# The output product of a second FFN by seven products instead of eight, with its weights stationary

## Chip, cores, metric

One core of one Trainium2 chip. The metric is the device time of one execution in microseconds (us); the kernel before has a median of 1644.6 us.

## What is computed

A linear attention with a normalised output gives x of 4608 tokens x 512. Two feed-forward networks follow, each 512 to 2048 to 512, in float32. The change touches the second:

```python
def _moe2_ref(x, w_in, w_out):
    h = x @ w_in                      # (4608, 512) @ (512, 2048)
    beta = 1.0
    neg = h <= -beta
    pos = h >= beta
    g = np.where(pos, h, np.where(neg, 0.0, (h + beta) ** 2 / (4.0 * beta)))
    return (g @ w_out).astype(np.float32)   # (4608, 2048) @ (2048, 512)
```

## The kernel before

Tokens go in nine blocks of T = 512, the 2048 hidden columns in NF = 16 steps f of 128, eight pairs i of two steps. Every float32 product is made of three matmuls on float32r parts: an operand is split into hi (a ScalarE copy, rounded) and lo (a VectorE subtraction), and hi x hi, hi x lo and lo x hi are added in PSUM.

Nothing is issued in the order of the source. `op` (line 61) records each operation with its engine, a cost in us and a key; `new` (184) takes a tile from a ring of a fixed number of buffers, and a tile's operations wait for those of the tile that had its buffer. `Program.order` (78 to 128) then simulates the five queues (PE, ACT, DVE, POOL and SP, which issues all DMAs): a free engine starts the ready operation with the smallest key, and the kernel is written out in that order. PE's three matmuls are planned at 0.68 us, a VectorE operation C_TT at 0.602, a ScalarE one C_SB at 0.52, and after a DMA's issue cost 2.1 us pass.

In the first FFN (`ffn_step` with ph = 0, nine blocks) VectorE also decodes the 64-bit weights of the second FFN's first product (`prepare`, 314), forms the four sums S1 to S4 of their quarters for Strassen's scheme and stores all eight as tiles of 128 x 512 (256 hi columns, 256 lo) in DRAM (`wd`). Block 0 of the second FFN is done plainly (`ffn_step`, ph = 1): its first-product weights are fetched from `wd` (`fetch`, 660), its output weights decoded by `weight` (286) into the rings woh and wol, where they stay to the end.

The other eight blocks go in four groups g of two blocks ja and jb. `x_combinations` (669) loads x of both, forms and splits seven combinations (B11, T2, T1, B21, T3, T4, B22; 22 VectorE and 14 ScalarE operations, 10 loads). `ffn2_pair` (720) makes the h of two steps f and both blocks with seven products of six matmuls each into the banks h, o, m (Winograd's form: v1, u2, u3 gather the sums), its seven weight tiles streamed through the ring wih of 16. `ffn2_group` (788) applies `nonlinear` (761) to the four results, splits g into gh and gl, and multiplies with the resident weights by `ffn2_out` (772): for each f and each block four chunks of 128 tokens, g stationary, the weights moving, three matmuls each, summed over f in the banks acc0 to acc3. Since only four banks hold sums, the results of one block wait in ring raw while the other is summed, and the sums are made in halves of f (`partial`). Each result block of 128 tokens x 512 columns is stored in one DMA of 2 KB rows (`out_block`).

## Time and profile before

| what | value |
|---|---|
| median of three runs | 1644.6 us (1644.13 to 1646.16) |
| profiled execution | 1641.85 us, its span 1640.0 us |
| PE busy, matmuls | 1613.8 us (98%), 7696 |
| DVE, ACT busy | 1233.3 us (75%), 1100.8 us (67%) |
| moved by DMA | 180.34 MB, mean 110 GB/s |
| second FFN, four groups | from about 968 us to the end |

PE is TensorE's matmuls, PEld its weight loads, DVE VectorE, ACT ScalarE, SP the queue that issues DMAs (SPq). Times are us from the start of the span. [...] The duration of a matmul or an engine's operation includes its latency, and following ones overlap with it.

### The profile page before, as it was taken

The numbers are of one execution on the slowest core, as the hardware profiler recorded it, in microseconds if no ns is written. First come the engines' busy times: TensorE is split into PE (matmuls) and PEld (weight loads), VectorE is DVE, ScalarE is ACT, GpSimd is POOL, SyncE is SP. The second block draws the span as 40 slices with busy tenths as digits, with TensorE's granted clock in tenths as the row PEclk, the third lists the DMA queues.
The fourth block names the chain that finished last, engine by engine and source line by source line (L and its number), as shares of the span: only waits on it lengthen the run. The fifth ranks groups of instructions, "written<-read, shape, count | busy, mean of one in ns | idle before, by whom it ended". The sixth has DMA issues, their size and how long they took to land.

```text
span 1640.0 us, 21677 instructions
## 1 busy us (share of the span) xinstructions
PE 1613.8 (98%) x7696; PEld 1297.9 (79%) x7696; DVE 1233.3 (75%) x1968; ACT 1100.8 (67%) x1881; POOL 0.2 (0%) x4
## 2 busy tenths in 40 slices
PE   6999999999999999999999999999999999999999
PEld 3665788888888888888888878888888888888887
DVE  5999999999999999999999734346534653465343
ACT  6988888888888888888888635345434543454343
POOL 0000000000000000000000000000000000000000
PEclk9999999999999999999999999999999999999999
DMA  8966303030211203021434644235423542344211
GB/s 276 308 213 201 129 27 110 20 116 21 76 41 46 89 27 109 14 90 39 148 109 151 211 139 127 79 103 167 126 80 102 166 126 82 101 137 128 78 33 52
DMA packets 107116, 180.34 MB, mean 110 GB/s; under 512 B 18240, under 2 KB 42688, under 8 KB 107008
## 3 DMA queue, kind: packets, MB, share of 16 engines
q1 hardware_dynamic: 107008, 178.96, 34.8%
q8 instruction: 61, 1.00, 0.3%
q14 instruction: 47, 0.39, 0.1%
HBM read 142.35 MB, written 36.57 MB: 109 GB/s over the span
## 4 chain that ended last, share of the span: by engine, by line
PE 84%; DVE 7%; ACT 4%; DMA 3%; issue 1%; SPq 0%; ACTq 0%; DVEq 0%
PE h L586 7%; PE o L735 7%; PE h L587 7%; PE h L588 7%; PE acc L782 7%; PE acc L784 7%; PE acc L783 7%; PE acc L635 6%; PE acc L636 6%; PE acc L637 6%; PE h L735 5%; PE m L735 5%; PE acc L633 2%; DVE u L212 1%; DMA io<-x2d 1%; DMA raw<-in_w_dram 1%
## 5 line engine op out<-in xcount | busy, mean ns | idle before, releaser
L586 PE MATMUL h<-xh,wih 128*128 128x512 f32 x640 | 256.8, 401 | 4.0 <-DVE t L212 2.0
L587 PE MATMUL h<-xl,wih 128*128 128x512 f32 x640 | 249.3, 389 | 0.0
L588 PE MATMUL h<-xh,wil 128*128 128x512 f32 x576 | 224.3, 389 | 0.0
L782 PE MATMUL acc<-woh,gh 128*128 128x512 f32 x512 | 199.5, 390 | 1.5 <-ACT ah L198 1.5
L635 PE MATMUL acc<-gh,woh 128*128 128x512 f32 x512 | 200.0, 391 | 0.0
L636 PE MATMUL acc<-gh,wol 128*128 128x512 f32 x512 | 199.3, 389 | 0.0
L784 PE MATMUL acc<-woh,gl 128*128 128x512 f32 x512 | 199.2, 389 | 0.0
L783 PE MATMUL acc<-wol,gh 128*128 128x512 f32 x512 | 199.2, 389 | 0.0
L637 PE MATMUL acc<-gl,woh 128*128 128x512 f32 x512 | 199.2, 389 | 0.0
L212 DVE SCALAR_TENSOR_TENSOR u<-u,r 128x512 f32<-128x512 f32 x272 | 187.0, 688 | 2.1 <-ACT r L198 0.9
L203 DVE TENSOR_TENSOR gl<-u,gh 128x512 fp32r<-128x512 f32 x208 | 143.0, 689 | 41.5 <-ACT gh L198 33.6
L198 ACT ACTIVATE gh<-u 128x512 fp32r<-128x512 f32 x208 | 130.9, 631 | 64.1 <-PE acc L640 20.0
L586 PEld LDWEIGHTS h<-xh,wih 128*128 128x128 f32 x640 | 120.1, 188 | 36.4 <-DVE t L212 3.2
L587 PEld LDWEIGHTS h<-xl,wih 128*128 128x128 f32 x640 | 120.2, 188 | 27.1 <-issue 3.2
L198 ACT ACTIVATE r<-u 128x512 f32<-128x512 f32 x144 | 91.1, 633 | 65.6 <-DVE u L208 65.6
L588 PEld LDWEIGHTS h<-xh,wil 128*128 128x128 f32 x576 | 108.2, 188 | 22.8
L198 ACT ACTIVATE u<-ah,absb 128x512 f32<-128x512 f32 x144 | 117.7, 818 | 0.0
L198 ACT ACTIVATE u<-kv 128x512 f32<-128x512 f32 x64 | 40.4, 632 | 114.9 <-DVE kv L743 102.2
L782 PEld LDWEIGHTS acc<-woh,gh 128*128 128x128 f32 x512 | 96.1, 188 | 22.5 <-ACT ah L198 2.7
L635 PEld LDWEIGHTS acc<-gh,woh 128*128 128x128 f32 x512 | 96.1, 188 | 21.4 <-ACT ah L198 1.0
L784 PEld LDWEIGHTS acc<-woh,gl 128*128 128x128 f32 x512 | 96.1, 188 | 20.1 <-DVE gl L203 0.2
L198 ACT ACTIVATE t<-h,na 128x512 f32<-128x512 f32 x144 | 112.0, 778 | 0.0
(163 smaller groups left out, 3107.5 us busy)
## 6 DMA issues: line engine op xcount, KB each, us to landing
wih<-wd SPq DMA_DIRECT2D x256, 256.0 KB, 2.8
raw<-in_w_dram SPq DMA_DIRECT2D x64, 512.0 KB, 4.3
wd<-raw SPq DMA_DIRECT2D x48, 256.0 KB, 2.2
io<-x2d SPq DMA_DIRECT2D x44, 256.0 KB, 2.9
x2d<-io SPq DMA_DIRECT2D x36, 256.0 KB, 2.3
raw<-in_qT_dram SPq DMA_DIRECT2D x56, 128.0 KB, 3.0
raw<-in_kv_dram SPq DMA_DIRECT2D x12, 512.0 KB, 5.0
out_dram<-a SPq DMA_DIRECT2D x18, 256.0 KB, 2.1
```

The source lines that it names most:

```text
L198: op(ACT, cost, key, lambda: nc.scalar.activation(out=out(), in_=in_(), func=func, **{k: v() if callable(v) else v for k, v in kw.items()} ...
L212: op(DVE, C_STT if callable(add) else C_TT, key, lambda: nc.vector.scalar_tensor_tensor(out=out(), in0=x(), scalar=add() if callable(add) ...
L586: nc.tensor.matmul(out=h(), lhsT=whi()[:, hc], rhs=xh(), start=(p == 0), stop=False)
L587: nc.tensor.matmul(out=h(), lhsT=whi()[:, hc], rhs=xl(), start=False, stop=False)
L588: nc.tensor.matmul(out=h(), lhsT=wlo()[:, lc], rhs=xh(), start=False, stop=(p == KT - 1))
L635: nc.tensor.matmul(out=o(), lhsT=wohi()[:, c], rhs=gh(), start=first, stop=False)
L636: nc.tensor.matmul(out=o(), lhsT=wolo()[:, c], rhs=gh(), start=False, stop=False)
L637: nc.tensor.matmul(out=o(), lhsT=wohi()[:, c], rhs=gl(), start=False, stop=last)
L735: nc.tensor.matmul(out=bank(), lhsT=l, rhs=r[k](), start=(start and k == 0 and m == 0), stop=(k == 1 and m == 2), skip_group_check=True,)
L782: nc.tensor.matmul(out=o(), lhsT=gh()[:, c], rhs=wohi(), start=first, stop=False)
L783: nc.tensor.matmul(out=o(), lhsT=gh()[:, c], rhs=wolo(), start=False, stop=False)
L784: nc.tensor.matmul(out=o(), lhsT=gl()[:, c], rhs=wohi(), start=False, stop=last)
```

## The change

In the four groups the second product is made by the same scheme as the first. Over the pairs i, the two steps f of a pair and the two halves of the 512 output columns are the quarters of the weights; the two blocks and the two steps are the quarters of g. So all eight pairs' g are kept: `ffn2_in` now ends with the four results of a pair in ring slots of woh and wol (the plain block's weights are no longer needed there), as B11, T1, T2 and B21. `ffn2_out` runs after all eight `ffn2_in` of the group: seven products, each over eight pairs with two halves of 128 output columns, the weights stationary and streamed from a new DRAM tensor `wod`, hi and lo of the g combination moving (made from the kept g just before, in ring raw; T3, B22 and T4 are formed anew each time in ring dec). The result comes out with columns on partitions and tokens along them; `put` turns it in squares of 32 x 32 on VectorE and stores it in four DMAs of 32 partitions. For the squares to join up, the output columns of the weights are permuted (`swapped`, `straight`), and the plain block's result is put back by its PSUM copy.

`prepare_out` takes the place of `weight(1, f, 1, ...)`: it decodes two steps' output weights, splits them as before, stores A11, A12 and A22 from the parts, forms and splits S1 to S4 and stores these. Ring wil gets 12 instead of 16 buffers; two tiles of a new ring ow hold the first four steps' lo of the first FFN and later the turned results. The combinations of x get keys spread over a longer stretch. The rest of the removed code (`ffn2_pair`, `ffn2_group`, the old `ffn2_out`, `stream`) is in the listing above. The diff, cut to its core:

```diff
+    wod = dram.tile([NPAIR, 8, P, T], F32, name="wod")
-        "wih": NF, "wil": NF, "woh": NF, "wol": NF + 1, "raw": 4, "dec": 2, "io": 3, "xh": KT, "xl": KT,
+        "wih": NF, "wil": NF - 4, "ow": 2, "woh": NF, "wol": NF + 1, "raw": 4, "dec": 2, "io": 3, "xh": KT, "xl": KT,
...
+    def swapped(x, h=None):
+        x = x.rearrange("p (a m j) -> p m a j", a=4, m=4)
+        return x if h is None else x[:, 2 * h:2 * h + 2]
+    def straight(x, m=4):
+        return x.rearrange("p (m a j) -> p m a j", m=m, a=4)
+    def prepare_out(i, key):
+        ts, his, los = [], [], []
+        for n in range(2):
+            f, k = 2 * i + n, key + n
+            raw, t = new("raw", k, I64, (P, DM)), new("dec", k, I32)
+            hi, lo = new("woh", k, F32R), new("wol", k, F32R)
+            load(k - 4, raw, w2[f, 1], 1.4)
+            decode(k, raw, t, new(f"kv{n}", 0.5 * (k - NS1) - 20 + NS1, I32))
+            op(ACT, C_SB, k, lambda t=t, hi=hi: nc.scalar.activation(
+                out=straight(hi()), in_=swapped(t().bitcast(F32)), func=AF.Copy), [t], [hi])
+            op(DVE, C_TT, k, lambda t=t, hi=hi, lo=lo: nc.vector.tensor_tensor(
+                out=straight(lo()), in0=swapped(t().bitcast(F32)), in1=straight(hi().bitcast(F32)), op=ALU.subtract
+            ), [t, hi], [lo])
+            wsb[1, f, 1] = (hi, lo)
+            ts.append(t)
+            cs = (A11, A21) if n == 0 else (A12, A22)
+            done = prog.buf(None)
+            def go(hi=hi, lo=lo, cs=cs, n=n):
+                for h in range(n + 1):
+                    for o, x in ((0, hi), (HW, lo)):
+                        nc.sync.dma_start(out=wod[i, cs[h], :, o:o + HW], in_=x().bitcast(F32)[:, h * HW:(h + 1) * HW])
+            op(SP, 0.7 * (n + 1), k + 1.5, go, [hi, lo], [done])
+            for c in cs[:n + 1]:
+                wods[i, c] = done
...
+        k = key + 2
+        s12, s34 = new("a1", k), new("a2", k)
+        (a, b), q = ts, (slice(0, HW), slice(HW, T))
...
+        def add(out, oh, x, y, alu, reads):
+            op(DVE, 0.34, k, lambda: nc.vector.tensor_tensor(
+                out=half(out, oh), in0=x(), in1=y(), op=alu), reads, [out])
+        add(s12, 0, lambda: whole(a, 1), lambda: whole(b, 1), ALU.add, [a, b])
+        add(s12, 1, lambda: half(s12, 0), lambda: whole(a, 0), ALU.subtract, [s12, a])
+        add(s34, 0, lambda: whole(a, 0), lambda: whole(a, 1), ALU.subtract, [a])
+        add(s34, 1, lambda: whole(b, 0), lambda: half(s12, 1), ALU.subtract, [b, s12])
+        for t, ring, c in ((s12, "a3", S1), (s34, "a4", S3)):
+            hi = new(ring, k, F32R)
+            op(ACT, C_SB, k + 0.5, lambda t=t, hi=hi: nc.scalar.activation(
+                out=hi(), in_=t(), func=AF.Copy), [t], [hi])
+            op(DVE, C_TT, k + 0.5, lambda t=t, hi=hi: nc.vector.tensor_tensor(
+                out=t().bitcast(F32R), in0=t(), in1=hi().bitcast(F32), op=ALU.subtract
+            ), [t, hi], [t])
...
-                t = new(("r", "r", "a1", "a2")[m] if ph else "io", k)
-                activate(k, t, o, cost=C_PS)
+                t = new("ow" if ph else "io", k)
+                if ph:
+                    op(ACT, C_PS, k, lambda t=t, o=o: nc.scalar.activation(
+                        out=swapped(t()), in_=straight(o()), func=AF.Copy), [o], [t])
+                else:
+                    activate(k, t, o, cost=C_PS)
...
+    PRODUCTS = ((0, A11, B11), (1, S2, T2), (2, S1, T1), (1, S3, T3), (0, A12, B21), (2, S4, B22), (1, A22, T4))
+    PAIR, PROD = 1.75, 2.0
...
+    def x_combinations(g, key, span):
...
+        at = [0]
+        def now():
+            at[0] += 1
+            return key + span * at[0] / 22
...
+    def pe_product(cost, key, bank, w, m, hi, lo, start, stop):
+        def mm():
+            wh, wl = (w()[:, o + m * P:o + (m + 1) * P] for o in (0, HW))
+            for n, (l, r) in enumerate(((wh, hi), (wh, lo), (wl, hi))):
+                nc.tensor.matmul(
+                    out=bank(), lhsT=l, rhs=r(), start=(start and n == 0), stop=(stop and n == 2), skip_group_check=True,
+                )
+        op(PE, cost, key, mm, [w, hi, lo], [bank])
...
+    def ffn2_in(g, i, key):
+        odd = (i + (g == 0)) % 2
+        a, b, c = banks = [new(r, key) for r in ("h", ("acc0", "o")[odd], ("acc1", "m")[odd])]
+        v1, u2, u3 = new("t", key), new(("kv0", "a1")[odd], key), new(("kv1", "a2")[odd], key)
+        def product(n):
+            bank, wc, xn = PRODUCTS[n]
+            w = fetch(wd, wds, i, wc, key - 4 + 0.1 * n, 4)
+            for k in range(2):
+                pe_product(0.68, key + 0.1 * n, banks[bank], w, k, xc[g, xn][0][k], xc[g, xn][1][k], n < 3 and k == 0, k == 1)
+        product(0)
+        activate(key, v1, a, cost=C_PS)
+        product(1)
+        arith(key, u2, v1, b)
+        product(2)
+        product(3)
+        arith(key, u3, v1, b)
+        product(4)
+        arith(key, u3, u3, c)
+        product(5)
+        product(6)
+        k = key + 0.8
+        g11, g12 = (new("woh", k + 0.1 * n) for n in range(2))
+        g22, g21 = (new("wol", k + 0.1 * n) for n in range(2))
+        nonlinear(a, g11, k)
+        nonlinear(u3, g22, k)
+        arith(key, u2, u2, c)
+        arith(key, v1, v1, b)
+        nonlinear(u2, g12, k)
+        nonlinear(v1, g21, k)
+        arith(k + 0.2, g12, g12, g11, ALU.subtract)
+        arith(k + 0.2, g22, g22, g12, ALU.subtract)
+        return {B11: g11, T1: g12, T2: g22, B21: g21}
...
+    def ffn2_out(g, gs, key):
+        banks = [[new(r, key + PROD * n) for r in rs]
+                 for n, rs in enumerate((("acc2", "acc3"), ("o", "m"), ("acc0", "acc1")))]
+        v1, u2, u3 = [[new(r, key + PROD * n) for r in rs]
+                      for n, rs in enumerate((("a3", "a4"), ("gh", "gh"), ("gl", "gl")))]
+        def product(n):
+            bank, wc, xn = PRODUCTS[n]
+            for i in range(NPAIR):
+                k = key + PROD * n + PROD / NPAIR * i
+                w = fetch(wod, wods, i, wc, k - 4, 4)
+                x = new("raw", k - 0.5, F32R, (P, 2 * T))
+                hi, lo = Half(x, slice(0, T)), Half(x, slice(T, 2 * T))
+                e, ke = gs[i].get(xn), k - 0.6
+                if e is None:
+                    l, r, alu = {T3: (T2, B11, ALU.subtract), B22: (T2, T1, ALU.add), T4: (B21, T2, ALU.subtract)}[xn]
+                    l, r, e = gs[i][l], gs[i][r], new("dec", k - 0.5)
+                    op(DVE, C_TT, ke, lambda l=l, r=r, e=e, alu=alu: nc.vector.tensor_tensor(
+                        out=e(), in0=l(), in1=r(), op=alu), [l, r], [e])
+                op(ACT, C_SB, ke, lambda e=e, hi=hi: nc.scalar.activation(
+                    out=hi(), in_=e(), func=AF.Copy), [e], [hi])
+                op(DVE, C_TT, ke, lambda e=e, hi=hi, lo=lo: nc.vector.tensor_tensor(
+                    out=lo(), in0=e(), in1=hi().bitcast(F32), op=ALU.subtract), [e, hi], [lo])
+                for m in range(2):
+                    pe_product(0.68, k, banks[bank][m], w, m, hi, lo, n < 3 and i == 0, i == NPAIR - 1)
+            return key + PROD * (n + 1)
+        def put(j, h, cs, key):
+            w = new("ow", key, shape=(P, 2 * T))
+            for m in range(2):
+                op(DVE, C_TT, key, lambda m=m: nc.vector.transpose(
+                    out=w().rearrange("p (b m j) -> p m b j", m=2, j=32)[:, m], in_=cs[m]()), [cs[m]], [w])
+            stored = prog.buf(None)
+            def go():
+                for n in range(4):
+                    nc.sync.dma_start(
+                        out=out[j * T:(j + 1) * T, n * P + h * D:n * P + (h + 1) * D].rearrange("(b i) c -> i b c", i=32),
+                        in_=w()[n * 32:(n + 1) * 32].rearrange("p (b c) -> p b c", c=D),
+                    )
+            op(SP, 2.8, key, go, [w], [stored])
...
+        a, b, c = banks
+        k = product(0)
+        for m in range(2):
+            activate(k, v1[m], a[m], cost=C_PS)
+        k = product(1)
+        for m in range(2):
+            arith(k, u2[m], v1[m], b[m])
+        product(2)
+        k = product(3)
+        for m in range(2):
+            arith(k, u3[m], v1[m], b[m])
+        for m in range(2):
+            arith(k, u3[m], u3[m], c[m])
+        put(jb, 1, u3, k + 1)
+        k = product(4)
+        put(ja, 0, a, k)
+        k = product(5)
+        for m in range(2):
+            arith(k, u2[m], u2[m], c[m])
+        put(jb, 0, u2, k + 1)
+        k = product(6)
+        for m in range(2):
+            arith(k, v1[m], v1[m], b[m])
+        put(ja, 1, v1, k + 0.5)
...
-        weight(1, f, 1, NS1 + f - 0.95 + 2.9)
+        if f % 2 == 0:
+            prepare_out(f // 2, NS1 + f - 0.5)
         for n in range(2):
-            plain[f, n] = fetch(f // 2, (A11, A21)[f % 2] + n, NS1 + f - 3 + 0.4 * n, 0)
+            plain[f, n] = fetch(wd, wds, f // 2, (A11, A21)[f % 2] + n, NS1 + f - 3 + 0.4 * n, 0)
...
-        s0 = NS1 + NF + 2 * NF * g
-        x_combinations(g, s0 - 6)
-        for i in range(NPAIR):
-            stream(g, i, s0 + (i // 4) * NF + 2.92 * (i % 4) - 7)
-        ffn2_group(g, s0)
+        s0 = NS1 + NF + (NPAIR * PAIR + 7 * PROD) * g
+        x_combinations(g, s0 - (8 if g else 6), 6 if g else 4)
+        units = [ffn2_in(g, i, s0 + PAIR * i) for i in range(NPAIR)]
+        ffn2_out(g, units, s0 + NPAIR * PAIR)
```

## Rows read from the trace of the kernel before

**Rows 1.** The page's busy times (us, share of the span, instructions).

```profile
PE 1613.8 (98%) x7696; PEld 1297.9 (79%) x7696; DVE 1233.3 (75%) x1968; ACT 1100.8 (67%) x1881; POOL 0.2 (0%) x4
```

**Rows 2.** The page's chain that ended last, by engine.

```profile
PE 84%; DVE 7%; ACT 4%; DMA 3%; issue 1%; SPq 0%; ACTq 0%; DVEq 0%
```

**Rows 3.** Stage windows, the groups: length; busy us (instructions) by engine; clock; DMA share, GB/s.

```profile
968.00:1114.00 146.00, 144.86 (x639) 119.54 (x638) 70.42 (x106) 64.38 (x109) 0.00 (x0) 1.00 0.41 119
1114.00:1278.00 164.00, 163.38 (x722) 134.95 (x721) 85.02 (x131) 74.13 (x127) 0.00 (x0) 1.00 0.41 119
1278.00:1442.00 164.00, 163.13 (x720) 134.78 (x719) 84.80 (x130) 73.89 (x126) 0.00 (x0) 1.00 0.40 119
1442.00:1606.00 164.00, 164.00 (x725) 135.51 (x724) 80.28 (x123) 71.25 (x122) 0.00 (x0) 1.00 0.29 86
```

**Rows 4.** Waits of PE from 960 us on: us in total, times, longest.

```profile
PE acc L782 <- ACT ah L198: 1.5, 2, 0.9
PE o L735 <- DVE kv L743: 1.1, 1, 1.1
```

**Rows 5.** Chain in order of time: start, us, what (two pieces of a group).

```profile
1154.61 1.36 PE h L735 x6
1155.97 1.36 PE o L735 x6
```

**Rows 6.** Groups of instructions, second FFN's matmuls: count, busy us, mean ns, idle before.

```profile
L782 PE MATMUL acc<-woh,gh 128*128 128x512 f32 x512 | 199.5, 390 | 1.5 <-ACT ah L198 1.5
...
L735 PE MATMUL o<-xh,wih 128*128 128x512 f32 x256 | 89.3, 390 | 1.1 <-DVE kv L743 1.1
...
L735 PE MATMUL m<-xl,wih 128*128 128x512 f32 x64 | 24.9, 389 | 0.0
```

**Rows 7.** Timeline of DVE, first FFN: start, us, line, operation.

```profile
312.17 0.69 DVE L203 TENSOR_TENSOR gl<-u,gh 128x512 fp32r<-128x512 f32 x1
312.77 0.68 DVE L212 SCALAR_TENSOR_TENSOR u<-u,r 128x512 f32<-128x512 f32 x1
...
320.71 0.42 DVE L331 TENSOR_TENSOR raw<-dec 128x256 f32<-128x256 f32 x1
321.05 0.75 DVE L212 SCALAR_TENSOR_TENSOR r<-t,na,r 128x512 f32<-128x512 f32 x1
```

**Rows 8.** A window of the first FFN, columns as in rows 3.

```profile
270.00:360.00 90.00, 90.00 (x428) 73.73 (x427) 87.78 (x143) 76.37 (x131) 0.00 (x0) 1.00 0.18 59
```

**Rows 9.** SP's issues by line: ns min/median/max; landing likewise, us (of line 662).

```profile
L662 SPq DMA_DIRECT2D wih<-wd x256: 319/320/1270, 798.6 to 1570.8; - x128
DMA to landing us min/median/max: 2.3/2.8/5.1
...
L434 SPq DMA_DIRECT2D kv<-kvd x28: 512/602/612, 121.7 to 584.1; - x28
```

**Rows 10.** Windows with the fullest DMA and with kv's reload, columns as in rows 3.

```profile
60.00:80.00 20.00, 20.00 (x137) 12.73 (x135) 20.00 (x33) 19.91 (x38) 0.00 (x0) 1.00 0.99 330
...
311.00:312.00 1.00, 1.00 (x6) 0.83 (x5) 1.00 (x3) 1.00 (x3) 0.00 (x0) 1.00 0.48 106
```

**Rows 11.** Timeline at the end of the span, all engines.

```profile
1634.14 2.73 DVE L840 TENSOR_TENSOR a<-a,acc 128x512 f32<-128x512 f32 x4 [2.27 <-PE acc L784]
...
1634.85 2.37 SPq L799 DMA_DIRECT2D out_dram<-a x4
...
1635.75 0.39 PE L784 MATMUL acc<-woh,gl 128*128 128x512 f32 x1
```

**Rows 12.** Windows around the plain block, columns as in rows 3.

```profile
880.00:900.00 20.00, 20.00 (x90) 16.57 (x89) 17.95 (x30) 15.98 (x29) 0.00 (x0) 1.00 0.61 185
900.00:920.00 20.00, 19.08 (x85) 15.48 (x84) 18.50 (x30) 16.36 (x31) 0.00 (x0) 1.00 0.81 271
920.00:940.00 20.00, 20.00 (x90) 16.57 (x89) 13.75 (x22) 11.62 (x20) 0.00 (x0) 1.00 0.58 176
940.00:960.00 20.00, 20.00 (x90) 16.58 (x89) 4.85 (x7) 6.83 (x11) 0.00 (x0) 1.00 0.36 105
```

More of the change, by code (lines that the diff above doesn't have):

```diff
@@ L679, in x_combinations @@
             k = key + 0.1 * n
-            hl = [[new("wil", k + 6 + 0.01 * (2 * m + i), F32R) for i in range(2)] for m in range(2)]
-            xc[g, c] = hl
+            xc[g, c] = [[new("wil", k + 0.01 * (2 * m + i), F32R) for i in range(2)] for m in range(2)]
         for n, c in enumerate((B21, T3, T4, B22)):
@@ L684, in x_combinations, with read, sub @@
             xc[g, c] = [[Half(w, slice(i * T, (i + 1) * T)) for i in range(2)] for w in wholes]
+        at = [0]
+        def now():
+            at[0] += 1
+            return key + span * at[0] / 22
+        def read(j, p):
+            k = key + span * at[0] / 22
+            t = new("io", k)
+            load(k - 1, t, x2d[j, p], reads=[x2s[j, p]])
+            return t
+        def sub(out, x, y):
+            op(DVE, C_TT, now(), lambda: nc.vector.tensor_tensor(
+                out=out(), in0=x(), in1=y(), op=ALU.subtract), [x, y], [out])
@@ L698, in split @@
-            def split(c, e, i=i, k=k):
-                x_split(e, xc[g, c][0][i], xc[g, c][1][i], k + 0.01 * c)
-            b11, b12 = fetch(ja, i, 0), fetch(jb, i, 1)
-            split(B11, b11)
-            t1, t2 = (new("dec", k + 6 + 0.1 * n) for n in range(2))
+            b11, b12 = read(ja, i), read(jb, i)
+            split(B11, b11, i)
+            t1, t2 = (new("r", key + i + 0.1 * n) for n in range(2))
             sub(t1, b12, b11)
-            b22 = fetch(jb, 2 + i, 2)
+            b22 = read(jb, 2 + i)
@@ L706, in x_combinations @@
             sub(t2, b22, t1)
-            split(T2, t2)
-            split(T1, t1)
-            b21 = fetch(ja, 2 + i, 3)
-            split(B21, b21)
+            split(T2, t2, i)
+            split(T1, t1, i)
+            b21 = read(ja, 2 + i)
+            split(B21, b21, i)
             sub(b12, b22, b12)
-            split(T3, b12)
-            t4 = new(f"kv{i}", k + 4)
+            split(T3, b12, i)
+            t4 = new("t", key + 1 + 0.1 * i)
             sub(t4, b21, t2)
-            late.append((split, fetch, t4))
@@ L716, in x_combinations @@
-        for i, (split, fetch, t4) in enumerate(late):
-            split(T4, t4)
-            split(B22, fetch(jb, 2 + i, 4))
-    def ffn2_pair(g, i, key):
-        banks = [new(r, key) for r in ("h", "o", "m")]
-        a, b, c = banks
-        v1, u2, u3 = new("t", key), new("kv0", key), new("kv1", key)
-        def product(n, bank, wc, xn, start):
-            w = ws[g, i, wc]
-            xh, xl = xc[g, xn]
-            def mm():
-                for k in range(2):
-                    hi, lo = (w()[:, o + k * P:o + (k + 1) * P] for o in (0, HW))
-                    for m, (l, r) in enumerate(((hi, xh), (hi, xl), (lo, xh))):
-                        nc.tensor.matmul(
-                            out=bank(), lhsT=l, rhs=r[k](), start=(start and k == 0 and m == 0),
-                            stop=(k == 1 and m == 2), skip_group_check=True,
-                        )
-            op(PE, 1.36, key + 0.01 * n, mm, [w, *xh, *xl], [bank])
-        def add(out, x, bank):
-            op(DVE, C_TT, key, lambda: nc.vector.tensor_tensor(
-                out=out(), in0=x(), in1=bank(), op=ALU.add), [x, bank], [out])
-        product(0, a, A11, B11, True)
-        product(1, b, S2, T2, True)
-        product(2, c, S1, T1, True)
-        activate(key, v1, a, cost=C_PS)
-        add(u2, v1, b)
-        product(3, a, A12, B21, False)
-        product(4, b, S3, T3, False)
-        add(u3, v1, b)
-        add(u3, u3, c)
-        product(5, b, A22, T4, False)
-        product(6, c, S4, B22, False)
-        add(v1, v1, b)
-        add(u2, u2, c)
-        return (a, u2), (v1, u3)
@@ new lines, in x_combinations @@
+            late.append(t4)
+        for i, t4 in enumerate(late):
+            split(T4, t4, i)
+            split(B22, read(jb, 2 + i), i)
+    def pe_product(cost, key, bank, w, m, hi, lo, start, stop):
[6 more added lines that the diff above has]
+        op(PE, cost, key, mm, [w, hi, lo], [bank])
@@ L770, in nonlinear @@
         return out
-    def ffn2_out(e, f, o4, key, first, last):
-        gh, gl = new("gh", key - 0.8, F32R), new("gl", key - 0.8, F32R)
-        activate(key - 0.8, gh, e)
-        subtract(key - 0.8, gl, e, gh)
-        wohi, wolo = wsb[1, f, 1]
-        for m in range(4):
-            o = o4[m]
-            def out_mm(m=m, o=o):
-                c = slice(m * P, (m + 1) * P)
-                nc.tensor.matmul(out=o(), lhsT=gh()[:, c], rhs=wohi(), start=first, stop=False)
-                nc.tensor.matmul(out=o(), lhsT=gh()[:, c], rhs=wolo(), start=False, stop=False)
-                nc.tensor.matmul(out=o(), lhsT=gl()[:, c], rhs=wohi(), start=False, stop=last)
-            op(PE, 0.68, key, out_mm, [wohi, wolo, gh, gl], [o])
@@ L851 @@
     for f, half in order:
-        weight(0, f, half, early.get((f, half), f - 2.8 + half * 2.7))
+        weight(f, half, early.get((f, half), f - 2.8 + half * 2.7))
     kv_batch(0, -30, 0.01)
```

118 lines of the change are left out of this document (40 added, 78 removed).

## Prediction

> **What bounds the kernel now.** I read the busy shares first: PE is busy 98% of the span [rows 1]. The chain that ended last says the same, PE 84%, DVE 7% [rows 2]. Then the stages: in the four groups of two token blocks (968 us to the end) PE has 144.86 of 146, 163.38 of 164, 163.13 of 164 and 164.00 of 164 us, while DVE has 70 to 85 and ACT 64 to 74 [rows 3]. The view of PE's waits from 960 us on has two lines, 2.6 us together [rows 4]. So in the stage that the change rewrites nothing but the number of matmuls sets the time, and what one costs is read from the chain: six take 1.36 us, 0.2267 us each [rows 5]. (The mean of 390 ns in a group row is latency; they overlap.)
>
> **Matmuls, the gain.** A group now does 8 pairs x 7 products x 6 = 336 matmuls of the first product (nine groups of line 735, 1344 = 4 x 336) and 16 rows of g x 2 blocks x 4 x 3 = 384 of the second (lines 782 to 784, 3 x 512 = 4 x 384) [rows 6]. The change makes the second 7 products x 8 pairs x 2 halves x 3 = 336. That is 48 fewer in each group, 192 x 0.2267 = **43.5 us**, all on the path that sets the end. A group's PE work is then 672 x 0.2267 = 152.3 us, half first product, half second (76.2 each).
>
> **VectorE in a group.** Durations of 0.69 us overlap too; ops that follow without a gap start 0.60 us apart [rows 7]. Before, a group has 130 of them: 8 x 13 in the pairs, 4 for the partial sums, 22 in x_combinations. The change drops 32 (gl) and 4, adds 56 (lo of each unit of pair and product), 24 (T3, B22, T4 are not kept), 16 (g12 and g22 by differences), 10 for the banks and 8 transposes: 208 x 0.603 = 125.4 of 152.3 us. In the first half it is 88 ops, 53 of 76 us. In the second half, with the 22 for the next group, 120 ops, 72.4 of 76.2 us: 95%. That can be carried: from 270 to 360 us PE was busy all 90 us with DVE at 87.8 of 90 [rows 8], under the same planner. Its costs are near the trace's: 0.68 for three matmuls (0.680), 0.602 for a VectorE op. ScalarE goes from 126 to 144 ops; at 73.9/126 = 0.59 us each [rows 3] that is 85 of 152 us, no bound.
>
> The transpose stands nowhere in this trace. [...] I take a full op, 0.603, since it moves the same 128x512 elements. [...]
>
> Price of stalls: the second half buffers four units ahead (ring raw, 4), 5.4 us, and the waits on a bank have a whole product (10.9 us) between writer and reader. In the first half c must be read between products 3 and 5, two VectorE ops in 1.36 us, but the planner puts products of the next pair there, whose banks alternate. Loads of x2 come later than planned on a fuller queue. Before lost 0.0 to 1.1 us per group; I take 1.25, **5 us** in all, between 0 and the DVE rival below.
>
> **Streams.** Each group fetches 112 tiles of 256 KB instead of 56, one per 1.36 us. With 2.6 MB of x2 and 2.1 MB of results that is 34.1 MB in 152.3 us, 224 GB/s; 119 GB/s cost a share of 0.41 [rows 3], so 0.77. The queue issues one in 0.32 us and it lands in 2.8 [rows 9]; the ring wih holds 16 tiles, 21.8 us ahead. Hidden, at zero, while a fetch is less than 20 us late.
>
> **Stores.** Eight stores of 128 rows of 2 KB per group become 16 of 32 partitions, each of 512 pieces of 256 B. The nearest row is the reload of kv in 256 B pieces: 0.60 us per issue [rows 9], 106 GB/s at a share of 0.48 [rows 10], a full-share rate of 221 GB/s. A put of 512 KB is then 2.4 us of the engines and 2.4 us of SP's queue; upper bound 1.2 us per issue (double pieces), 4.8. All fetches queued behind wait that long, far less than 20 us. But that row reads DRAM; a write to DRAM in 256 B pieces is not in the trace. [...]
>
> **The tail.** Now the last matmul starts at 1635.75 and the span ends at 1640.0: 4.25 us [rows 11]. After, both banks of the last product end together: VectorE adds twice and transposes twice (last one done 0.43 + 3 x 0.603 + 0.09 = 2.3 us after that start), then four issues of 0.60 (the fourth starts 1.9 later), 2.2 us to land as now, 0.9 to the end: 7.3. With 1.2 us per issue and 5 us of landing, 12. Growth 3 to 8, I take **5**.
>
> **The plain block (about 895 to 968 us).** prepare_out adds per pair two full and four half VectorE ops, 8 x (2 x 0.603 + 4 x 0.34) = 20.5 us, and two ScalarE ops. From 880 to 960 DVE has 55.1 of 80 us [rows 12], so 75.6: it fits. Its DMAs are the tighter part: seven tiles per pair, 56 x 256 KB = 14.7 MB in 1 KB rows, on top of the 14.7 MB that those 80 us move now (mean 184 GB/s): 368 GB/s, more than the 330 GB/s seen at a share of 0.99 [rows 10]. 3.0 MB, 9 us, spill. They may: the stores are read only in group 0's second half, 76 us on, and the plain fetches run up to 16 tiles (43 us) ahead. What is queued behind on SP are weight loads, and an ACT decode that waits for a late one holds the nonlinear op behind it, then PE. Between 0 and 9, I take **3**. Group 0's x combinations share VectorE with this, and are late next.
>
> At nothing: the wider "ow" tiles and the ring wil of 12 in the first FFN (the early weights only change homes, and its stage is bound by PE and DVE at 90.0 and 87.8 of 90 [rows 8]); "ow" for the plain block's four results (two wait for a store, while acc2 and acc3 are next needed 76 us later).
>
> **The sum.** The profiled execution takes 1641.85 us (span 1640.0); it lies 2.75 under the median of the runs, 1644.6. 1641.85 - 43.5 + 5 + 5 + 3 = 1611.4; on the median, **1614**.
>
> **Rivals.**
> 1. VectorE bounds the second half. If the 22 combination ops stay where their keys put them (s0-8, the last four products), these products carry 32 + 24 + 22 + 12 = 90 ops, 54.3 us, against 43.5 of PE: 10.8 over, less up to 5.4 of buffer, in three groups: 16 to 32 us, 1624 to 1645, centre 1632. For it: DVE at 95%, late x2 loads, dear transposes. Against: the planner starts any ready operation on an idle engine, and in the first three products VectorE has 24 x (1.36 - 0.60) = 18 us free for 13.3 of combinations.
> 2. The plain block starves: the 9 us of spill and a disordered queue stop PE, and group 0 starts late by VectorE as well: 10 to 20 us beyond the sum, 1621 to 1631. For it [rows 10, 12]; against, the look-ahead.
> 3. Stores of 256 B pieces saturate the DMA engines; slower than before. Without the puts a group wants 32 MB, at 290 GB/s 110 of 152 us; 42 us are left, 10.5 per put (50 GB/s). Beyond that point every us counts four times per group; at 13.5 us per put (39 GB/s) 4 x 12 = 48 us, 1662. Against it is the 221 GB/s of the reload.
> 4. It doesn't do what it says (PE stalls eat the 48 matmuls): 1641 to 1648. Against it: PE's order is planned with costs that match.
>
> **How the numbers follow.** Forecast 0.66, rival 1 0.18, rival 2 0.08, rival 3 0.05, rival 4 0.03. The forecast's own range is 1602 (only 3 us of tail lost, and a little less than now of waits) to 1624. The 8-in-10 range reaches into rivals 1 and 2: 1602 to 1637. A measurement of this kernel tells 0.2%, 3.3 us, from no change. Faster: 0.66 + 0.16 + 0.08 = 0.90; same 0.03; slower 0.07.
>
> **What would show it.** PE count 7504 and the six still 1.36 us apart; groups of 152 to 155 us; DVE near 80% over a group, with no stretch of the second half where PE waits for lo (rival 1); PE waits near 900 to 975 us for ACT or DMA (rival 2); landing of the 256 B stores under 6 us, and fetches not later than about 10 (rival 3); last matmul 7 to 12 us before the end. Wrong if PE waits for wih, or for VectorE, over more than 20 us.

## Result and profile after

The changed kernel takes 1603.8 us (median of four runs, 1603.2 to 1604.2) against 1644.4 (1642.7 to 1646.2) for the kernel before: a ratio of 0.975, interval 0.974 to 0.977. Its profiled execution took 1604.24 us, span 1602.5. Between the medians that is 40.5 us less, between the two profiled executions 37.6.

First the page's busy times and its chain by engine, kernel after:

```profile
PE 1573.0 (98%) x7504; PEld 1261.1 (79%) x7504; DVE 1438.7 (90%) x2328; ACT 1145.5 (71%) x1969; POOL 0.2 (0%) x4
...
PE 92%; ACT 3%; DMA 3%; DVE 1%; issue 0%; SPq 0%; DVEq 0%; ACTq 0%
```

Against [rows 1, 2] there are 192 matmuls fewer, as counted, and DVE rises from 75% to 90%; yet the chain has PE for 92% (84% before) and DVE for 1% (7% before). VectorE got fuller and all but left the chain that ended last.

The groups, each cut into its two halves (windows: length; busy us and instructions of PE, PEld, DVE, ACT, POOL; the granted TensorE clock, 1.00 at full speed; DMA share, GB/s):

```profile
1061.00:1137.50 76.50, 76.50 (x339) 63.38 (x338) 70.39 (x114) 39.76 (x67) 0.00 (x0) 1.00 0.78 239
1137.50:1213.50 76.00, 76.00 (x335) 62.32 (x334) 60.56 (x95) 44.00 (x77) 0.00 (x0) 1.00 0.69 208
1213.50:1289.80 76.30, 76.30 (x339) 63.16 (x338) 69.79 (x114) 39.77 (x67) 0.00 (x0) 1.00 0.81 241
...
1518.30:1594.50 76.20, 76.20 (x337) 62.91 (x336) 61.13 (x96) 35.78 (x59) 0.00 (x0) 1.00 0.59 166
```

PE is busy for the whole of every half, which [rows 3] could not say of three groups of four. A first half has about 60 us of DVE, a second with the next group's combinations 70 of 76, the last one without them 61. The view of PE's waits from 880 us on (total, times, longest):

```profile
PE h L669 <- DVE u L820: 1.6, 1, 1.6
PE o L805 <- DVE a L812: 0.2, 1, 0.2
```

Both lie before 980 us, at the plain block and at the first pair. None is in the groups, where [rows 4] had 1.5 us. The timeline of DVE at the end of the first three groups (start, us, line, operation) gives their length:

```profile
1137.97 1.30 DVE L892 STREAM_TRANSPOSE ow<-a 128x512 f32<-128x512 f32 x2
...
1290.77 1.30 DVE L892 STREAM_TRANSPOSE ow<-a 128x512 f32<-128x512 f32 x2
...
1443.54 1.30 DVE L892 STREAM_TRANSPOSE ow<-a 128x512 f32<-128x512 f32 x2
```

152.8 us apart: 672 x 0.2267 = 152.3, and 0.5 us of delays. Before, the groups were 164 us [rows 3].

**Where the time went.** The last output matmul of the first FFN, the 4468th of all in both kernels, starts at 899.04 us before and at 900.93 after: 1.9 us of the profiled pair were lost ahead of the stage that the change rewrites. In the twelve traces of the changed kernel and of its variants below this matmul starts between 899.4 and 903.3 us, so the difference is no larger than what this stretch scatters; with one trace of the kernel before, a share of the change in it is neither shown nor excluded. From this matmul to the end it is 741.0 us before and 701.6 after, 39.4 less. A window of 90 us from it shows the plain block, before and then after:

```profile
899.04:989.04 90.00, 87.94 (x387) 72.20 (x386) 51.04 (x79) 46.47 (x81) 0.00 (x0) 1.00 0.54 169
```

```profile
900.93:990.93 90.00, 88.00 (x382) 70.93 (x381) 72.18 (x125) 59.15 (x106) 0.00 (x0) 1.00 0.91 301
```

The busy times are equal, the instructions are not: five matmuls fewer, 5 x 0.2267 = 1.1 us. A busy PE hid them, as the timeline of PE shows where DMA is fullest:

```profile
941.97 0.39 PE L671 MATMUL h<-xh,wih 128*128 128x512 f32 x1
942.31 0.50 PE L722 MATMUL acc<-woh,gh 128*128 128x512 f32 x1
942.65 0.40 PE L723 MATMUL acc<-wol,gh 128*128 128x512 f32 x1
943.11 0.50 PE L724 MATMUL acc<-woh,gl 128*128 128x512 f32 x1
```

They start 0.34 to 0.46 us apart instead of 0.227, too little to be shown as idle. The ledger of the profiled pair is then: matmuls -43.5; waits in the groups -1.5; the plain block +1.1; the tail +3.7 (below); the start +1.9. That is -38.3, and the spans differ by -37.5. The rest, 0.8 us, are delays too short to be shown as waits: from the 4468th matmul to the last, 736.7 us before hold 3228 pitches of 0.2267 us and 4.9 us more, and 693.6 us after hold 3036 pitches and 5.4 us more. Counted so, plain block and groups together changed by +0.5 us, not by 1.1 - 1.5 = -0.4, and the ledger closes.

### The profile page after: what moved, and what is told of

Same layout as the page of the kernel before. It is cut to its first block, busy times and chain, and to the rows that moved or that the text cites. A ratio compares the mean times of both kernels' runs of the same rounds, so it can differ in the third digit from the quotient of the medians.

```text
span 1602.5 us, 22540 instructions
## 1 busy us (share of the span) xinstructions
PE 1573.0 (98%) x7504; PEld 1261.1 (79%) x7504; DVE 1438.7 (90%) x2328; ACT 1145.5 (71%) x1969; POOL 0.2 (0%) x4
## 4 chain that ended last, share of the span: by engine, by line
PE 92%; ACT 3%; DMA 3%; DVE 1%; issue 0%; SPq 0%; DVEq 0%; ACTq 0%
PE acc L805 18%; PE h L669 9%; PE h L670 8%; PE h L671 8%; PE o L805 8%; PE acc L718 7%; PE acc L719 7%; PE acc L720 7%; PE m L805 7%; PE h L805 5%; PE acc L716 2%; DMA io<-x2d 1%; PE m L474 1%; DMA wol<-in_kv_dram 1%; DMA raw<-in_w_dram 1%; PE o L619 1%
## 5 line engine op out<-in xcount | busy, mean ns | idle before, releaser
L805 PE MATMUL acc<-raw,wih 128*128 128x512 f32 x768 | 176.2, 389 | 0.0
L671 PE MATMUL h<-xh,wil 128*128 128x512 f32 x432 | 168.2, 389 | 0.0
L805 PEld LDWEIGHTS acc<-raw,wih 128*128 128x128 f32 x768 | 144.2, 188 | 29.9
L881 ACT ACTIVATE raw<-dec 128x512 fp32r<-128x512 f32 x96 | 60.1, 633 | 81.3 <-DVE dec L879 43.1
L720 PEld LDWEIGHTS acc<-gl,woh 128*128 128x128 f32 x512 | 96.1, 188 | 20.0
L719 PEld LDWEIGHTS acc<-gh,wol 128*128 128x128 f32 x512 | 96.1, 188 | 19.7
L213 DVE SCALAR_TENSOR_TENSOR r<-t,na,r 128x512 f32<-128x512 f32 x144 | 107.3, 745 | 0.9
L213 DVE SCALAR_TENSOR_TENSOR t<-t,na,h 128x512 f32<-128x512 f32 x144 | 106.5, 740 | 0.2
L199 ACT ACTIVATE gh<-u 128x512 fp32r<-128x512 f32 x144 | 90.8, 631 | 21.9 <-DVE u L213 16.0
L199 ACT ACTIVATE ah<-h 128x512 f32<-128x512 f32 x144 | 85.4, 593 | 22.7 <-PE h L671 22.1
```

Source lines behind the costliest of these rows:

```text
L199: op(ACT, cost, key, lambda: nc.scalar.activation(out=out(), in_=in_(), func=func, **{k: v() if callable(v) else v for k, v in kw.items()} ...
L213: op(DVE, C_STT if callable(add) else C_TT, key, lambda: nc.vector.scalar_tensor_tensor(out=out(), in0=x(), scalar=add() if callable(add) ...
L671: nc.tensor.matmul(out=h(), lhsT=wlo()[:, lc], rhs=xh(), start=False, stop=(p == KT - 1))
L719: nc.tensor.matmul(out=o(), lhsT=wolo()[:, c], rhs=gh(), start=False, stop=False)
L720: nc.tensor.matmul(out=o(), lhsT=wohi()[:, c], rhs=gl(), start=False, stop=last)
L805: nc.tensor.matmul(out=bank(), lhsT=l, rhs=r(), start=(start and n == 0), stop=(stop and n == 2), skip_group_check=True,)
```

## Experiments

Each kernel is the changed one with one edit; times are medians, and "more" or "less" is against the 1603.8 us of the changed kernel. Ratios are against the kernel before, run again beside each experiment (medians of 1643.4 to 1644.4 us).

**1. The combinations of x kept late.** Rival 1 of the prediction needs them in the last products of a second half. In the changed kernel's second group the 22 operations run at 1203 to 1241 us, around the change from the first half to the second (at about 1214). Here they can't start before the third product is done.

```diff
-            load(k - 1, t, x2d[j, p], reads=[x2s[j, p]])
+            load(k - 1, t, x2d[j, p], reads=[x2s[j, p], opened[g - 1]] if g else [x2s[j, p]])
...
         product(2)
+        opened[g] = prog.buf(None)
+        op(PE, 0.0, key + 3 * PROD, lambda: None, [c[1]], [opened[g]])
```

> The loads of x for the next group's combinations are held back until the third product of the second half is done, so that the 22 VectorE operations fall into its last four products, in three groups (the first group's stay). Theory P (VectorE binds where a stretch holds more of its work than matmuls): those products then carry 90 operations, 54.3 us, against 43.5 us of matmuls; less up to 5.4 us of buffer that is 5 to 11 us per group, 1620 to 1637 us in all, with PE waiting for lo parts (raw) and for the combinations (wil, xh). Rival W (the buffer and work of the next group hide it): under 1608 us.

1622.6 us (1618.6 to 1626.0), ratio 0.987. A window in the second half of group 1:

```profile
1247.00:1299.00 52.00, 47.82 (x202) 37.19 (x202) 49.31 (x81) 27.60 (x47) 0.00 (x0) 1.00 0.80 241
```

DVE has 49 of 52 us, and PE loses 4.2. PE's waits from 960 us on are now mostly waits for the moving operand (tile raw); the third line is the bank h, which ScalarE has still to read:

```profile
PE acc L806 <- ACT raw L882: 5.4, 6, 1.4
PE acc L806 <- DVE raw L884: 4.6, 10, 0.6
PE h L806 <- ACT t L199: 3.8, 3, 1.8
```

So rival 1 is a real mechanism of 19 us (16 to 32 were forecast for it), and what keeps it away is the place that the planner gives these 22 operations.

**2. More VectorE work in the second half.** A copy of 32 kept operands per group (the maximum of a tile with itself), 32 x 0.603 = 19.3 us.

```diff
                         out=e(), in0=l(), in1=r(), op=alu), [l, r], [e])
+                else:
+                    e0, e = e, new("dec", k - 0.5)
+                    arith(ke, e, e0, e0, ALU.max)
```

> 32 more VectorE operations per group in the second half: where a kept combination of g is used as it is, it is first passed through an elementwise maximum with itself, which changes no value. Theory P (each half has its own budget): 152 operations x 0.603 = 91.7 us against 76.2 us of matmuls in three groups, 130 operations, 78.4 us, in the last; 10 to 15 us per group, 1632 to 1652 us. Rival W (the slack is that of the whole group, 240 x 0.603 = 144.7 of 152.3 us): under 1610 us.

1638.4 us (1634.8 to 1639.9), ratio 0.996: 34.6 us more. 70 + 19 = 89 us of VectorE don't fit into 76, and most of the change's gain is gone.

**3. The same amount in the first half.** Four maxima per pair, again 19.3 us per group.

```diff
         arith(k + 0.2, g22, g22, g12, ALU.subtract)
+        for t in (g11, g12, g22, g21):
+            arith(k + 0.2, t, t, t, ALU.max)
```

> The same 32 more VectorE operations per group, but in the first half: four per pair, each a maximum of a kept g with itself. Theory P: 120 x 0.603 = 72.4 us against 76.2 us of matmuls, so within 3 us of the changed kernel, 1603 to 1607 us. Rival W: the same as for the dose in the second half, whatever that gives; a theory by which any further VectorE work costs its length would give 1604 + 4 x 32 x 0.603 = 1681 us.

1622.2 us (1620.6 to 1625.6), ratio 0.987: 18.3 us more, where nothing was expected. The budget of the half was read too coarsely: its 60 us of DVE and these 19 make 79 of 76, and the excess cannot be put off for long, since the products of the second half need the last pairs' g. Two windows at the change of halves and the waits of PE:

```profile
1213.00:1223.00 10.00, 10.00 (x45) 8.28 (x45) 10.00 (x18) 8.17 (x15) 0.00 (x0) 1.00 0.74 214
1223.00:1233.00 10.00, 6.44 (x26) 4.48 (x25) 10.00 (x17) 4.58 (x8) 0.00 (x0) 1.00 0.51 152
```

```profile
PE acc L805 <- DVE raw L885: 7.3, 8, 1.6
PE acc L805 <- ACT raw L883: 5.5, 4, 1.4
```

In the changed kernel itself these windows are full on VectorE already, and PE just keeps up:

```profile
1207.50:1217.50 10.00, 10.00 (x45) 8.25 (x45) 9.96 (x17) 7.39 (x15) 0.00 (x0) 1.00 0.77 224
1217.50:1227.50 10.00, 10.00 (x46) 8.28 (x45) 10.00 (x18) 8.25 (x17) 0.00 (x0) 1.00 0.85 268
```

A part of the 18.3 us is not VectorE's work but the granted clock. In the third group PE waits in the same place, and in the 10 us after that the clock is 0.83 in the mean: 38 matmuls run where 45 or 46 would, about 1.6 us.

```profile
1380.00:1390.00 10.00, 6.48 (x26) 4.51 (x25) 10.00 (x17) 4.60 (x8) 0.00 (x0) 1.00 0.48 148
1390.00:1400.00 10.00, 10.00 (x38) 8.03 (x37) 8.28 (x15) 6.18 (x11) 0.00 (x0) 0.83 0.54 170
```

The fourth group shows the same behind its waits (0.90 and 0.93 in the windows from 1540 to 1560 us); in the second group the clock stays at 1.00.

**4 and 5. Half of that dose, by place.** Either the half's size decides, or how near to the change of halves the work lies. The same edit for pairs 0 to 3 alone (`if i < 4`), and for pairs 4 to 7 alone (`if i > 3`), 9.6 us per group each.

```diff
+        for t in (g11, g12, g22, g21) if i < 4 else ():
+            arith(k + 0.2, t, t, t, ALU.max)
```

> The dose in the first half had cost 18 us where its own budget had room (72.4 of 76.2 us). Half of it now, 16 more VectorE operations per group, all in the pairs 0 to 3, none in 4 to 7. New theory T (what binds is the 20 us around the change from the first half to the second, where VectorE was already busy all the time in the changed kernel: the last pairs' work comes after their matmuls, with the lo parts and combinations of the second half behind it): under 3 us more than the changed kernel, 1603 to 1607 us. Rival S (95% of a half is simply too much, wherever in it the work lies): half of the 18 us, about 1613 us.

> The same 16 more VectorE operations per group, all in the pairs 4 to 7 of the first half. Theory T: nearly all of what the full dose of 32 cost, 12 to 18 us more than the changed kernel, 1616 to 1622 us, with PE waiting for VectorE within 15 us after the change of halves. Rival S: about 1613 us, as for the early pairs.

Early: 1605.0 us (1602.9 to 1607.5), ratio 0.976, groups of 152.7: nothing that can be told from no change. Late: 1611.3 us (1609.9 to 1613.5), ratio 0.980, 7.4 us more. That is less than theory T expected (12 to 18) and near the 1613 of rival S, but S expected the same for the early pairs, where it failed. The windows at the change of halves with the late dose:

```profile
1219.00:1229.00 10.00, 9.49 (x42) 7.29 (x40) 10.00 (x18) 6.25 (x12) 0.00 (x0) 1.00 0.72 197
1229.00:1249.00 20.00, 19.42 (x85) 15.83 (x86) 19.40 (x33) 13.70 (x24) 0.00 (x0) 1.00 0.75 232
```

The same 9.6 us cost nothing in one place and 7.4 us of the whole time in the other, so place decides: for some 20 us around the change of halves VectorE has no slack. Both halves of the dose together cost 18.3, more than 1.1 + 7.4. The trace shows the same by groups: the second and third are 157.2 and 158.8 us long with the whole dose, 155.0 and 154.5 with the late half, 152.7 with the early one. About 3 us of the difference are the two stretches at a lower clock (an estimate from the matmuls missing in the windows above); that the early part also eats the lead with which the late part is absorbed would fit, but no run separates it, and the size stays open.

**6. The stores of 256 B pieces.** The same tiles stored as 4 KB contiguous per partition; the arrangement of the output is left out.

```diff
-                        out=out[j * T:(j + 1) * T, n * P + h * D:n * P + (h + 1) * D].rearrange("(b i) c -> i b c", i=32),
-                        in_=w()[n * 32:(n + 1) * 32].rearrange("p (b c) -> p b c", c=D),
+                        out=out[j * T + h * 256 + n * 64:j * T + h * 256 + (n + 1) * 64].rearrange("(p r) c -> p (r c)", r=2),
+                        in_=w()[n * 32:(n + 1) * 32],
```

> The turned results are stored by the same 64 DMAs of 32 partitions, but each partition's 4 KB goes to one contiguous place instead of 16 pieces of 256 B, so the arrangement of the output is left out. If pieces of 256 B cost nothing on the path but in the tail (the forecast): 1 to 2.5 us less, 1601.5 to 1603 us, and a lower DMA share around the stores. If small writes hold back the fetches behind them (the third rival, in small): more than 4 us less.

1604.4 us (1603.8 to 1606.2), ratio 0.976: no difference, where 1 to 2.5 us less were forecast. From the third group's last turn to the end of the span it is 158.0 us (1444.55 to 1602.5) against 159.0 (1443.54 to 1602.5), so the tail alone is 1.0 us shorter. It doesn't show in the whole time because PE lost more in the plain block of this trace, which the edit doesn't touch (96.44 us busy from 880 to 980 us, against 98.00). In the groups the small pieces cost nothing: the third group is 152.8 us long here too (last turns at 1291.78 and 1444.55). Rival 3 is out.

**7. A shorter tail.** One bank of the last product is finished six matmuls earlier, so that its addition and turn run beside PE, and the last four DMAs go through two queues.

```diff
+                if n == 6 and i == NPAIR - 2 and 2 * g + 3 == NB:
+                    calls[0]()
+                    held = calls[1]
+                    continue
...
+                op(SP, 1.4, key, lambda: go((0, 1), nc.sync), [w], [stored])
+                op(ACT, 1.4, key, lambda: go((2, 3), nc.scalar), [w], [prog.buf(None)])
```

> Only the last store of the last group is changed: the last product's second-to-last unit does its second half after the last unit's first half, so that one bank ends 1.36 us before the other, and the four DMAs are issued by two queues, two each. From the changed kernel's tail (last matmul to the end of the span 7.9 us): one addition and one transpose less behind the last matmul, 1.2 us, and two issues of 0.55 us less, 1.1 us: 1601.5 us. If the transfer of the 512 KB is what takes the tail (3 us at some 170 GB/s): only the 1.2 us, 1602.6 us.

1604.7 us (1603.7 to 1606.6), ratio 0.976: no gain, where 1.2 or 2.3 us were forecast. The timeline at its end, and two windows of the last transfers:

```profile
1598.32 0.69 DVE L814 TENSOR_TENSOR a<-a,m 128x512 f32<-128x512 f32 x1
1599.04 0.71 DVE L905 STREAM_TRANSPOSE ow<-a 128x512 f32<-128x512 f32 x1
1599.78 0.85 SPq L911 DMA_DIRECT2D out_dram<-ow  x2
1599.78 0.93 ACTq L911 DMA_DIRECT2D out_dram<-ow  x2
```

```profile
1601.00:1602.00 1.00, 0.00 (x0) 0.00 (x0) 0.00 (x0) 0.00 (x0) 0.00 (x0) 1.00 1.06 209
1602.00:1603.00 1.00, 0.00 (x0) 0.00 (x0) 0.00 (x0) 0.00 (x0) 0.00 (x0) 1.00 1.01 197
```

The issues do run in parallel, but the transfer is then the limit: about 200 GB/s at a share of 1, 2.6 us for 512 KB. From the last matmul's start (1597.88) to the end it is 6.9 us instead of 7.9, and the last matmul itself came 0.6 us later after the third group's last turn (1446.26): the net is 0.4 us, within the scatter.

**8. The stores of the sums left out.** S1 to S4 of the output weights are not stored (their products then fetch other tiles): 32 x 256 KB less beside the plain block.

```diff
-            done = prog.buf(None)
+            continue
...
-                w = fetch(wod, wods, i, wc, k - 4, 4)
+                w = fetch(*((wod, wods) if (i, wc) in wods else (wd, wds)), i, wc, k - 4, 4)
```

> The stores of the four weight sums S1 to S4 in the plain block are left out (32 DMAs, 8.4 of 14.7 MB), and the four products that use them fetch the first FFN product's tiles in their place, so these products' values are left out. If the full DMA engines of the plain block cost what PE waits there (1.6 us for VectorE behind late loads of x): 1 to 3 us less, 1601 to 1603 us, and a DMA share well under 0.9 from 900 to 960 us. If they cost nothing: 1603.5 to 1604.5 us. If they also delay the first group: 4 us less or more.

1602.3 us (1601.5 to 1603.0), ratio 0.974, and PE's loss in the plain block is gone, with the DMA share at 0.71 (0.92 in the changed kernel, where PE has 98.00 us in this window):

```profile
880.00:980.00 100.00, 99.72 (x439) 81.90 (x438) 85.55 (x151) 70.27 (x124) 0.00 (x0) 1.00 0.71 235
```

**9. The plain block's loads of x.** The chain of the changed kernel (start, us, what) passes here through loads of x2:

```profile
936.07 5.01 DMA io<-x2d
...
944.93 5.02 DMA io<-x2d
949.97 0.64 ACT xh L199
950.63 0.69 DVE xl L204
...
952.53 0.61 DVE u L820
953.19 0.50 PE h L669
```

They take 5.0 us and are planned at 0.7 + 2.1. The last lines show how such a load reaches PE: the split of x (xh, xl) waits for it, and the operation that frees the bank h for PE (u, line 820) stands behind that split in VectorE's order. Here the planner is told 2.7 for those of group 0, and nothing else changes.

```diff
-            load(k - 1, t, x2d[j, p], reads=[x2s[j, p]])
+            load(k - 1, t, x2d[j, p], 0.7 if g else 2.7, reads=[x2s[j, p]])
```

> The planner is told that the first group's loads of x take 2.7 us of the queue instead of 0.7, nearer to what they take in the plain block while the DMA engines are full; nothing else is changed, only the order of work there. If the 1.6 us that PE waits in the plain block come from operations planned too early behind these loads: 1 to 2 us less than the changed kernel, 1602 to 1603 us. If they come from the full DMA engines themselves, whatever the order: no difference, or a later start of the first group, 1604 to 1606 us.

1601.2 us (1598.4 to 1603.9, five runs), ratio 0.9735, interval 0.9722 to 0.9749. The window shows what was gained; of the wait of 1.6 us nothing is left:

```profile
880.00:980.00 100.00, 99.60 (x440) 82.17 (x439) 83.88 (x147) 71.12 (x125) 0.00 (x0) 1.00 0.85 283
```

In the ten traces whose edits leave this stretch alone PE is idle for 1.1 to 3.6 of these 100 us; here it is 0.4, and 0.3 in experiment 8. The kernel does all the work and has the lowest median of those that do all of it; since its interval and the changed kernel's overlap, the 1.6 us that the trace shows is what may be claimed.

**10 and 11. Fewer matmuls.** To see whether PE still sets the time in both halves, the third matmul of every unit of the seventh product (lo of the weights by hi) is left out: 16 per group, 64 in all, 14.5 us. Once in `ffn2_in`, once in `ffn2_out`; `pe_product` gets a last argument for it, the number of matmuls. The call in `ffn2_in`:

```diff
-                pe_product(0.68, key + 0.1 * n, banks[bank], w, k, xc[g, xn][0][k], xc[g, xn][1][k], n < 3 and k == 0, k == 1)
+                pe_product(0.68, key + 0.1 * n, banks[bank], w, k, xc[g, xn][0][k], xc[g, xn][1][k], n < 3 and k == 0, k == 1, 2 if n == 6 else 3)
```

> In the first half's last product the third matmul of each split (lo of the weights times hi) is left out: 16 matmuls fewer per group, all else unchanged. Theory P (PE sets the time in this half; VectorE 53 of then 72.6 us): 64 x 0.2267 = 14.5 us less, 1589.3 us, within 1.5. If the second half or VectorE set the time, less than 7 us.

> The same 16 matmuls fewer per group, in the last product of the second half instead (lo of the weights times hi of T4 left out). There VectorE has 72.4 us of work against then 72.6 us of matmuls, and the last product alone carries two operations per unit and the previous arithmetic: 1.2 us per unit against 0.91 us of matmuls. Theory P with a budget by stretch: less is gained than in the first half, 4 to 11 us, 1593 to 1600 us. If VectorE has slack to spare here too: 14.5 us less, 1589.3 us.

In the first half: 1590.3 us (1588.2 to 1590.8), ratio 0.967, 13.5 us less; each matmul counts, and a group is 149.1 us long, 3.7 less. In the second: 1594.3 us (1591.8 to 1596.0), ratio 0.969, 9.6 us less, two thirds. The trace says where the last third went, and it is not where the expectation had it: a group is 149.2 us long here too (from the first group's last turn to the second's, and on to the third's), so 16 x 0.2267 = 3.6 us are gained in full. While VectorE prepares the shorter units of the seventh product, PE takes matmuls of the next group in between (VectorE adds to a bank of the next group's first pair, kv<-t,acc, at 1283.05 us, before it adds the seventh product's banks at 1285.33). Only in the fourth group there are none left, and there alone `PE o` waits for VectorE's lo, 1.3 us in three waits:

```profile
1577.15 0.50 PE L806 MATMUL o<-raw,wih 128*128 128x512 f32 x1 [0.55 <-DVE raw L884]
...
1580.15 0.50 PE L806 MATMUL o<-raw,wih 128*128 128x512 f32 x1 [0.55 <-DVE raw L884]
```

With the late starts around them that is about 3 us; another 1 us lies in the plain block of this trace, where the granted clock from 950 to 960 us is 0.83, after PE's wait. So PE still sets the time in both halves, and VectorE takes over only in the last product of all.

## Why the prediction was right, point by point

The measured 1603.8 us lie within the forecast's own range (1602 to 1624), near its lower end and 10 us under its centre of 1614. The gain from the matmuls came out as worked out; every charge set against it was too high: the stalls by 6.5 us, the tail by 1.3, the plain block by 1.9.

**What bounds it, and the matmuls: right.** PE bounded the groups before and bounds them after; a group is 152.8 us for 152.3 worked out, and the count is 7504. Experiment 10 finds 13.5 us for 64 matmuls where the pitch of [rows 5] gives 14.5, and in its trace 3.7 us per group for 16 where the pitch gives 3.6.

**VectorE: right in the total, and read too coarsely.** 208 operations of 0.603 us were counted, 125 us of a group; the two halves of the second group sum to 130 (60.6 + 69.8, durations of separate operations among them). The transpose was taken as a full operation, the author's estimate: single ones last 0.70 us and two in a row 1.30, so 0.60 from start to start, the value taken. What failed is the budget by halves: "95%, that can be carried" is true of the second half, but "53 of 76" suggested slack anywhere in the first half. Experiment 4 finds it in the first four pairs; experiments 3 and 5 don't find it near the change of halves.

**Stalls in the groups: mis-sized, 5 us taken.** The trace shows no wait of PE there, 1.5 us less than before. This is the largest part of why 1614 was too high. The sum also put the 5 us on top of a time that already held the waits of the kernel before. The four units of look-ahead and the waits on a bank with a whole product between were named as cover; they should have been believed down to nothing, and the charge for late x2 loads belonged to the plain block alone.

**Streams: right.** 207 to 241 GB/s in the halves for 224 worked out, shares of 0.67 to 0.81 for 0.77; in the last half, without loads of a next group, 166 GB/s at 0.59. No wait of PE for wih is in the list; the queue itself waits for free slots of the ring, 349 us from 980 us on, behind PE's matmuls. Landing, from the page's list of DMA issues:

```profile
wih<-wd SPq DMA_DIRECT2D x256, 256.0 KB, 2.9
wih<-wod SPq DMA_DIRECT2D x224, 256.0 KB, 3.0
...
out_dram<-ow SPq DMA_DIRECT2D x64, 128.0 KB, 3.1
```

**Stores: right that they don't bound, and the rate was near.** The reload of kv gave 221 GB/s at a full share [rows 10]; experiment 7 shows 197 to 209 for the writes, 0.89 to 0.95 of it. Such writes run below the 330 GB/s of [rows 10]. The size of the pieces is the smaller part of that, though. The last stores of the kernel before (2 KB rows, 128 partitions) and those of experiment 6 (4 KB pieces, 32 partitions) ran so:

```profile
1636.00:1638.00 2.00, 0.14 (x1) 0.00 (x0) 0.86 (x2) 0.00 (x0) 0.00 (x0) 1.00 1.00 378
1599.00:1600.50 1.50, 0.00 (x0) 0.00 (x0) 0.00 (x0) 0.00 (x0) 0.00 (x0) 0.50 0.96 254
```

With pieces of 4 KB most of the distance from 378 to some 200 GB/s is still there. That it comes from the 32 partitions of each DMA would fit, but no run separates it.

**The tail: 5 us taken, 3.7 measured.** The timeline after, all engines:

```profile
1594.12 0.86 PE L805 MATMUL m<-raw,wih 128*128 128x512 f32 x3
...
1595.01 0.69 DVE L812 TENSOR_TENSOR a<-a,m 128x512 f32<-128x512 f32 x1
1595.61 1.30 DVE L892 STREAM_TRANSPOSE ow<-a 128x512 f32<-128x512 f32 x2
1596.94 2.18 SPq L898 DMA_DIRECT2D out_dram<-ow  x4
```

The last of the three matmuls starts at 1594.12 + 2 x 0.227 = 1594.6, the span ends at 1602.5: 7.9 us for 7.3 worked out, against 4.25 before [rows 11]. The sum then took a rounded 5 rather than its own 3.

**The plain block: 3 us taken, 1.1 net.** The prediction's 0.34 us for a half-width VectorE operation is the distance from 320.71 to 321.05 in [rows 7]. The spill was right in kind: DMA is full, as the windows below show, and what was late is a load of x2 (5.0 us, planned 2.8), with the wait of 1.6 us behind it. What makes the small gaps at 942 no run shows; they come while DMA is full.

```profile
920.00:940.00 20.00, 20.00 (x89) 16.28 (x88) 18.05 (x33) 13.73 (x25) 0.00 (x0) 1.00 0.98 339
940.00:960.00 20.00, 18.17 (x77) 13.81 (x76) 16.92 (x30) 13.79 (x25) 0.00 (x0) 1.00 1.00 342
```

But the kernel before lost 2.1 us in the same stretch too (90 less 87.94; its two waits are in [rows 4, 12]), which the sum had left in. Experiments 8 and 9 remove the loss in two ways: fewer bytes, or an honest cost for the load.

**The rivals.** Rival 1 did not happen, for the reason given against it (the planner starts ready operations on an idle VectorE, here even 11 us before the second half begins), and experiment 1 shows that it would have cost 19 us. Rival 2 stayed at its beginning, 1.6 us. Rivals 3 and 4 are refuted by experiment 6 and by the groups' length.

With the terms as measured (-43.5 for the matmuls, +3.7 for the tail, +0.5 for plain block and groups together, -39.3 in all) the sum from the median before would have been 1644.4 - 39.3 = 1605.1, 1.3 us above the median measured; the start, which lay 1.9 us apart in the profiled pair, is left out of it.

## What to carry to other kernels

Here the bounding engine ran without gaps, and taking work from it gained the count times the pitch, less what the end of the kernel took back (43.5 less 3.7 us, with 40.5 measured between the medians); charges for stalls belonged only where a row shows a gap, in the 80 us in which another phase's transfers pile up (a wait of 1.6 us, at a DMA share of 1.00). VectorE at 90% was not to be judged by its mean over a stage but by the 20 us around the change of halves; a dose of dummy work, put in different places, measures the slack there (9.6 us per group cost 7.4 us near it and 1.1, no more than scatter, away from it). A short stretch in which another engine has more work than the bounding one (in experiment 11 a product of 1.2 us of VectorE against 0.91 of PE per unit) cost nothing where the bounding engine could take work of the next phase in between, and about 3 us at the very end, where there was none. And a planner's cost for a load that lands late under traffic can be raised in one stretch alone, which here took a wait of 1.6 us away without touching the work.

## What was not expected of the hardware

A PE that the windows show as 88.0 (after) and 87.9 us (before) busy of 90 executed 382 matmuls after and 387 before: matmuls of 0.39 us that start 0.34 instead of 0.227 us apart leave no gap in the record, so counts in equal windows tell what busy time does not. Behind 3.5 us of PE's waits within 10 us the granted clock of the next 10 us was 0.83 in one group of experiment 3 (38 matmuls instead of 45 or 46), while behind 3.6 us in another group it stayed at 1.00; no run shows what sets it. Writes to DRAM in 256 B pieces from 32 partitions ran at 197 to 209 GB/s with all DMA engines in use, close to reads of equal pieces (221, worked out from [rows 10]); in 4 KB pieces from 32 partitions they ran at 254, in 2 KB rows from 128 partitions at 378. And two queues that issue in parallel (0.85 and 0.93 us for two DMAs each, against 2.18 for four on one) brought the end only 1.0 us nearer: the transfer then took over as the limit, at shares of 1.06 and 1.01.
